# Transposes moved from TensorE to the DMA queue in a pooled-attention and mixture-of-experts kernel

## The chip, the core and the metric

The kernel runs on one core of a Trainium2 chip. The metric is the device time of one execution in microseconds, given as the median of the timed runs; one further execution was taken with the hardware profiler, and all rows of a profile come from it. In the profile PE is TensorE (PEld its weight loads), DVE is VectorE, ACT is ScalarE, POOL is GpSimd and SP is SyncE, which here does nothing but issue DMAs. "q" behind an engine's name (SPq) means its sequencer.

## The reference

Eight batches, 576 tokens each, 8 heads of 64. First attention over pooled keys: k and v are averaged over groups of 8 tokens, which leaves 72 of them. Its output x (512 wide) goes to a mixture of four attention experts with causal softmax, of which each token uses two.

```python
# attention over pooled k, v      (B, H, S, D) = (8, 8, 576, 64), pool = 8
k_p = k.reshape(B, H, Sp, pool, D).mean(axis=3)
v_p = v.reshape(B, H, Sp, pool, D).mean(axis=3)
attn = softmax(scale * q @ k_p.T)                  # 576 x 72 per head
x = (attn @ v_p) heads side by side                # (8, 576, 512)
# experts: E = 4, head width 64, the two best of four per token
logits = x @ w_gate
w = softmax of the two largest logits
for e in range(E):
    q, k, v = x @ wq[e], x @ wk[e], x @ wv[e]
    a = causal softmax(scale * q @ k.T)            # 576 x 576
    out += (w of e where e is among the two, else 0) * (a @ v @ wo[e])
```

## The kernel before

Each batch has 512 main tokens in four chunks of 128, and a tail of 64; the tails of two batches are worked on together. The work is cut into named units such as `5:x2` (batch 5, unit x2), each written as a Python generator, and `ORDER` (line 21) lists the units in the order in which they are emitted. A name that stands there twice or three times means the unit's next piece: usually PE's matmuls first, then the instruction that takes the result out of PSUM, then what follows (a mask, a store). Every instruction keeps its program order on its engine (`keep_in_program_order`, line 121, to which the profile therefore ascribes nearly everything), so each engine works through its own list, and an instruction that waits holds up all behind it on that engine. All DMAs are issued from SP's list, loads and stores alike. A DMA also waits until the DMA eight places ahead of it on that list has landed, since eight semaphores are used in turn.

The units that matter here:

- Loads `lk`, `lq`, `lv` (1 MB each per batch, two buffers of each) and the tails' loads `lkt`, `lqt`, `lvt`.
- `q0` to `q3` (`q_t`, line 357): four PE transposes of q per head pair into PSUM (`qT_ps`), one VectorE copy to `qT`. The main tokens lie with four consecutive tokens in one partition, and the transposes write into PSUM so that the order of the tokens is by chunk.
- `s0` to `s3` (`scores`, line 371): the scores against the pooled keys, and ScalarE's exponential into `etA`.
- `a0` to `a3` (`av`, line 384): the product with the pooled values into `oA_ps`, then on VectorE a reciprocal of the sums (`rzA`) and one multiplication for both heads that writes the chunk-wise `x_tm`.
- `x0` to `x3` (`x_t`, line 410): for every fourth column group `fc`, four PE transposes of x (with the permuted identity `perm`) into `xT_ps`, one VectorE copy of 128 x 512 into `xT`, which has two buffers.
- `p0` to `p3` (`proj`, line 458): the experts' q and k from `xT`; `v0` and `v2` (`values`, line 473): their v and the gate's logits.
- `g1` to `g6`: the gate. `g1` works on VectorE and ends with the mask of the two best; `g2` is one subtraction on POOL.
- `c00`, `c01`, `c10`, `c11`, `c2`: the experts' scores and their exponentials, with POOL's causal masks. `o0`, `o1` (`av`, line 607): the products with v for two experts each, and VectorE's scaling (`scaled`, line 547) into `o_sc`.
- `t0`, `t1` (`o_t`, line 633): four PE transposes of `o_sc` into `oT_ps` and one VectorE copy into `oT` (four buffers).
- `w0` to `w3`, `y0` to `y3` (`wo`, line 653): the output product from both `oT` of a batch, the copy from PSUM into one of three `ofin` buffers on ScalarE (w) or VectorE (y), and the store. `z0`, `z2` (`wo_two`, line 662) do the same for two chunks in the last batch.
- The tails' units: `qt`, `qx`, `sx`, `ax`, `xx`, `pt`, `vx`, `h0`, `h1`, `hd`, `ox`, `tx`, `w4`.
- `W:h0` to `W:h9` (`busy`, line 253): four matmuls on zeros whose result nobody reads.

At the start POOL zeroes four padded tiles, `etT`, two `etX` and `etD` (lines 198 to 200, through `persistent`, line 179), in which the tails' exponentials later fill only a part.

Of the kernel before, what the change touches and what calls it, by code (L numbers as in the profile page):

```python
# [21 lines left out]
0:lkb 0:lqb 0:lkt W:h6 W:h9 0:lvb W:h5 0:qcb1 0:ksb W:h2 0:lqa 0:kt 0:lva 0:qcb0 0:qca0 W:h3 W:h8  # L22
0:qca1 0:lvt 0:q3 0:q3 0:q2 0:lka 0:vsb W:h0 1:lkt 0:vsa 0:kpb 1:kt 0:q2 0:q1 0:kpb 0:q1 0:q0 1:lk
0:ksa 0:s2 0:kpa 0:q0 0:vt 0:kpa 0:vp 0:s2 1:lq 0:s1 0:s3 1:ks 1:qc W:lv 1:lv 0:vp 0:a2 W:h4 0:s1
0:a1 W:lq 0:a2 0:s3 0:a3 0:s0 1:kp W:h1 0:a1 0:s0 0:a3 0:a0 W:h7 1:kp 1:lvt 1:q2 0:a0 1:q0 1:q2 1:q0
0:lqt 1:q3 1:q1 1:q3 1:vs 1:s2 1:lqt 1:q1 1:s3 0:x1 0:x1 1:vt W:cv 0:x2 1:s0 0:x3 0:x2 1:qt 0:x3
1:s2 1:s0 0:x0 1:s3 1:s1 0:x0 0:v2 0:v2 0:v0 1:vp W:lk W:c2 2:lq 0:v0 1:vp 0:p2 0:g1 1:s1 W:c0 2:lkt
0:p2 1:a1 0:g2 2:lvt 1:a3 1:qx 2:lk 1:a2 W:c3 0:p0 1:a1 1:qx 2:lv 1:a3 W:c1 0:g3 1:a0 1:a2 0:p3 0:p0
1:sx 0:g4 0:g5 2:qc 0:p1 1:a0 0:p3 1:sx 0:c11 3:lq 0:c10 1:x2 0:p1 3:lkt 1:x1 1:x2 0:c11 1:x1 2:lqt
0:c2 1:x0 1:x0 1:x3 0:c10 1:ax 1:x3 2:q3 3:lqt 2:q3 3:lk 1:p2 2:kt 0:g6 0:c11 0:c2 2:vt 3:lv 0:c00  # L30
0:c01 2:q2 1:p2 0:c2 2:q0 0:c10 2:ks 0:c01 1:ax 2:q2 1:v0 2:q1 4:lkt 2:q0 1:v0 1:xx 0:o1 1:v2 2:q1
0:c01 1:xx 3:lvt 2:kp 1:v2 0:c00 2:kp 1:pt 0:o1 2:s0 2:s2 2:vs 1:vx 1:pt 2:s0 0:c00 0:t1 1:vx 1:g1
2:s1 2:s3 2:vp 0:t1 1:g2 2:s2 0:o0 1:p0 2:s3 2:vp 2:s1 3:kt 2:a3 2:a1 0:o0 2:a2 1:p0 3:qt 1:p3 1:p3
1:p1 2:a3 4:lq 3:qc 4:lk 2:a2 2:a1 2:a0 1:p1 1:c10 3:qx 1:c10 3:q1 2:a0 3:q1 3:ks 1:h1 3:qx 1:hd
2:x3 2:x2 1:h1 2:x3 2:x2 1:h0 1:hd 2:x0 2:x1 2:x0 1:c11 1:c00 3:vs 3:vt 2:x1 1:c10 3:q0 3:q3 3:q0
1:g3 1:h0 2:v0 1:g4 3:q3 3:kp 1:c11 3:kp 1:c00 2:v2 0:t0 3:s3 2:v0 0:t0 1:c2 3:q2 2:v2 3:q2 2:p0
1:c2 4:kt 3:vp 3:sx 2:p0 1:c01 2:p1 2:g1 3:s3 3:sx 5:lq 1:c01 3:vp 3:a3 1:hd 2:p2 3:ax 2:p1 3:a3
1:g5 2:p2 3:s1 3:s0 4:qc 1:c2 3:ax 4:q0 4:q0 1:g6 4:lv 3:s1 1:ox 4:lvt 1:ox 4:q1 1:c00 4:q1 3:s0
3:s2 3:s2 2:c01 4:ks 2:g2 1:c01 2:c00 4:q2 4:q2 3:xx W:lo 3:xx 3:a1 4:lqt 2:c01 3:a1 4:kp 3:pt 4:kp
3:a2 3:a2 2:c00 5:lkt 4:q3 3:a0 3:pt 1:o0 5:lqt 4:s1 5:lvt 2:p3 4:q3 3:a0 1:c11 3:x0 4:s1 2:p3 4:s0  # L40
4:s0 4:s2 5:qc 3:x1 1:o0 5:lk 3:x0 3:x1 4:s3 4:s3 5:q2 4:vs 4:vt 5:q2 1:t0 1:o1 5:vt 3:x3 2:g3 1:t0
3:x3 2:c2 3:x2 4:vp 3:x2 6:lvt 4:vp 2:c2 3:p1 1:o1 3:v0 2:c00 4:s2 2:c01 6:lkt 3:v0 5:lv 3:p1 5:q3
1:t1 2:c10 3:h0 1:t1 W:co 4:a1 2:c10 3:p3 4:a0 5:qt 5:q3 5:kt 3:p3 3:p2 3:p2 4:a1 5:qx 4:a0 2:c11
4:a3 5:q1 5:qx 2:g4 3:p0 3:h0 5:q1 4:a2 2:c10 2:c11 2:g5 0:w1 4:a3 3:p0 7:lkt 4:a2 3:c10 3:c11 5:ks
0:w1 5:kp 3:c10 4:x0 4:x0 3:v2 3:c11 5:kp 4:x2 4:x2 0:w0 2:c11 6:lq 2:c2 0:w0 3:c2 3:v2 5:s1 5:vs
# [12 lines left out]
4:g6 3:t1 5:g2 4:o1 7:s1 6:x2 7:qx 7:qx 4:o1 5:hd 5:h0 6:p2 7:q0 7:q0 7:sx 5:h1 5:c10 3:t0 6:p2 5:g3
7:sx 3:t0 6:p0 5:h1 7:a1 6:p3 6:v2 5:c10 4:o0 6:p3 1:w1 6:p1 7:a1 5:c10 6:v2 6:p0 3:tx 5:g4 7:a3
7:s0 4:o0 5:g5 3:tx 5:c2 6:p1 7:s0 3:y1 3:w4 7:a3 2:w1 2:w3 3:y1 7:ax 5:c2 7:a0 7:ax 3:w4 3:w0 7:a0  # L60
6:v0 3:y1 3:w0 3:w3 5:c00 5:g6 3:w3 7:x2 6:v0 5:c2 5:c01 7:x1 7:x2 7:x3 3:w4 5:c11 5:c00 7:x1 6:c10
4:t0 7:x3 5:c01 4:t0 5:c00 6:g1 5:ox 3:w0 7:xx 6:c2 5:c11 6:g2 6:c10 5:c01 5:c11 7:xx 6:c00 6:c2
7:vx 5:ox 5:o0 6:g3 7:vx 4:t1 4:t1 7:x0 6:c00 5:o1 7:x0 6:c10 4:w2 4:w2 7:p1 7:v0 5:o1 4:w2 5:o0
3:w3 7:p1 7:p3 4:y0 7:v0 7:p3 6:c11 6:c01 4:y0 4:y1 5:tx 6:c11 7:v2 6:c2 5:tx 3:w2 6:c01 4:y1 6:g4
7:p2 7:v2 6:c11 3:w2 6:c01 6:g5 7:p2 7:p0 6:g6 7:g1 5:t0 7:p0 7:c11 7:c10 6:c00 7:c10 5:t1 5:t0
7:c10 4:w3 6:o1 3:w2 5:t1 4:w3 7:c11 6:o0 7:g2 4:y0 5:w4 7:pt 6:o1 5:w4 5:y2 7:g3 7:c01 7:pt 6:o0
7:g4 4:y1 5:y2 7:c01 6:t0 6:t0 7:c2 6:t1 7:c2 7:g5 7:c11 7:g6 6:t1 4:w3 7:c2 5:y0 7:c00 5:w4 5:y0
5:y1 7:c00 7:h1 6:y1 5:y2 7:c01 5:y1 6:y1 5:y0 5:y1 7:c00 7:o1 7:h1 6:y1 6:w0 6:w0 7:o0 6:w0 5:w3
7:o1 7:t1 7:h0 5:w3 7:o0 7:hd 7:hd 7:t1 7:t0 7:h0 6:y3 7:t0 5:w3 7:z2 6:y3 7:hd 7:ox 6:y3 6:w2 7:z2
7:z0 7:ox 6:w2 7:tx 6:w2 7:tx 7:z0 7:w4 7:w4 7:w4  # L70
"""


@with_exitstack
def kernel(
# [103 lines left out]
    def persistent(name, count, shape, dtype, fills):  # L179
        bufs = []  # L180
        for i in range(count):
            t = const.tile(shape, dtype, name=f"{name}{i}")
            for pick, value in fills:
                nc.gpsimd.memset(pick(t), value)
            bufs.append(t)
        return bufs
# [82 lines left out]
    def part_a(b: int):  # L269
# [86 lines left out]

        def q_t(hp):
# [12 lines left out]

        def scores(hp):
            ps = ps2.tile([128, 2, MAIN], FP32, name="sA_ps", tag="ps2")
            for hh in range(2):
                r0 = hh * D
                pe.matmul(
                    out=ps[:, hh, :], lhsT=kp[r0 : r0 + D, hp, :],
                    rhs=st["qT"][r0 : r0 + D, hp, :], start=True, stop=True,
                )
            yield
            et = etp.tile([SP, 2, MAIN], BF16, name="etA", tag="etA")  # L380
            act.activation(out=et[:], in_=ps[0:SP, :, :], func=EXP, scale=ATT_EXP_SCALE)
            st["et"][hp] = et

        def av(hp):
# [4 lines left out]
            for hh in range(2):  # L389
# [10 lines left out]
            dve.reciprocal(out=rz[:], in_=view[:, :, :, D : D + 1])  # L400
            dve.tensor_tensor(
# [5 lines left out]
                op=MULT,  # L407
            )
# [31 lines left out]
        else:  # L440
# [5 lines left out]
            })  # L446
        units.update({f"{b}:{n}": f for n, f in names.items()})
# [4 lines left out]
    def part_p(b: int):  # L452
# [41 lines left out]
        def gate1():  # L494
# [72 lines left out]
    def part_s(b: int):  # L567
# [64 lines left out]

        def o_t(ep):
# [43 lines left out]
        for ep in range(NEP):  # L677
# [3 lines left out]
            names[f"t{ep}"] = lambda ep=ep: o_t(ep)  # L681
# [249 lines left out]
```

## Time and profile before

| | us |
|---|---|
| Median of 3 runs | 179.77 (179.53 to 181.32) |
| Profiled execution | 177.47 |
| its span from first to last instruction | 175.7 |
| TensorE's mean granted clock in it | 0.989 of full |

| What | Count | Mean, ns |
|---|---|---|
| PE transposes of x | 128 | 221 |
| PE transposes of the experts' output | 64 | 220 |
| VectorE copies into xT | 32 | 421 |
| VectorE copies into oT | 16 | 422 |
| POOL zeroing of etX, two tiles | 2 | 1906 |
| Stores of 256 KB, issue to landing | 28 | 2400 |

How to read it: the duration of a matmul in the profile is from its start to its modelled end, and matmuls follow each other much closer than that, so 221 ns is no price for a transpose. What a group of matmuls costs is read from the chain of waits or the timeline, where the next group's start shows when PE was free. "Idle before" is the time in which an engine had nothing to do ahead of an instruction, with what released it.

### The profile page before, as it was taken

What the parts mean: (1) busy time and instruction counts of PE and PEld (TensorE: products, weight loads), DVE (VectorE), ACT (ScalarE), POOL (GpSimd) and SP (SyncE); (2) the same over time, 40 slices, a digit from 0 to 9 for tenths busy, and PEclk for the clock granted to TensorE, in tenths of its full rate; (3) what the DMA queues carried; (4) which work ended last, traced back from release to release, by engine and by line L of the source; (5) the groups of instructions that cost most, each with busy time, mean ns of one, the idle gap of its engine ahead of it and who ended that gap; (6) DMA issues with size and microseconds to landing.
All of it is one profiled execution on the core that took longest, in us unless ns stands there. A gap on an engine that the chain in (4) does not pass through costs nothing.

```text
span 175.7 us, 5279 instructions
## 1 busy us (share of the span) xinstructions
PE 160.5 (91%) x2095; PEld 103.1 (59%) x2120; DVE 126.5 (72%) x357; ACT 124.1 (71%) x172; POOL 103.7 (59%) x212
## 2 busy tenths in 40 slices
PE   7849797999999999999999999999999999999680
PEld 2324455567667658676665687657666675575440
DVE  1586765867898767878777868786967877668650
ACT  2112647796669699787987798788796895798551
POOL 8963726369866999875789286982313171427000
PEclk9978999999999999999999999999999999999999
DMA  4999999999999999999947999352040503156566
GB/s 141 313 307 311 346 345 225 298 308 348 189 320 274 342 349 305 164 301 298 342 152 219 309 349 345 129 156 86 4 179 4 159 26 119 44 201 188 195 256 199
DMA packets 45208, 40.19 MB, mean 229 GB/s; under 512 B 14208, under 2 KB 40320, under 8 KB 45184
## 3 DMA queue, kind: packets, MB, share of 16 engines
q1 hardware_dynamic: 45184, 39.86, 78.1%
q8 instruction: 16, 0.26, 0.7%
q14 instruction: 8, 0.07, 0.1%
HBM read 30.42 MB, written 9.44 MB: 227 GB/s over the span
## 4 chain that ended last, share of the span: by engine, by line
PE 70%; SPq 12%; DMA 7%; ACT 5%; issue 2%; DVE 1%; POOL 0%; DVEq 0%; ACTq 0%; POOLq 0%
PE p_ps L121 16%; SPq L121 12%; PE v_ps L121 7%; PE y_ps L121 6%; PE sB_ps L121 6%; PE oB_ps L121 5%; DMA vtail<-in_v_dram 5%; PE oA_ps L121 4%; PE xT_ps L121 3%; PE sA_ps L121 3%; PE qT_ps L121 3%; PE oT_ps L121 3%; PE oBt_ps L121 2%; PE vp_ps L121 2%; PE pt_ps L121 2%
## 5 line engine op out<-in xcount | busy, mean ns | idle before, releaser
L121 ACT ACTIVATE etA<-sA_ps 72x1024 bf16<-72x1024 f32 x32 | 31.6, 1020 | 9.8 <-PE sA_ps L121 9.5
L121 ACT ACTIVATE etB<-sB_ps 128x1024 bf16<-128x1024 f32 x32 | 31.8, 1030 | 2.8 <-PE sB_ps L121 2.6
L121 PE MATMUL p_ps<-xT,wqk 128*128 128x512 bf16 x115 | 31.9, 379 | 0.8
L121 POOL TENSOR_SCALAR_AFFINE_SELECT etB<-etB 128x256 bf16<-128x256 bf16 x48 | 18.4, 406 | 21.2 <-ACT etB L121 21.0
L121 ACT CAST qk<-p_ps 128x512 bf16<-128x512 f32 x32 | 18.5, 586 | 10.8 <-PE p_ps L121 10.7
L121 POOL TENSOR_TENSOR vsum<-vraw 128x512 bf16<-128x512 f32 (+1 forms) x16 | 18.9, 1203 | 7.1 <-DMA vraw<-in_v_dram 5.3
L121 DVE TENSOR_TENSOR x_tm<-oA_ps,rzA 128x512 bf16<-128x512 f32 x32 | 22.1, 691 | 1.1
L121 PEld LDWEIGHTS <-wqk 128*128 128x128 bf16 x192 | 14.8, 98 | 9.7 <-issue 0.4
L121 POOL TENSOR_TENSOR ksum<-kraw 128x512 bf16<-128x512 f32 x14 | 17.5, 1271 | 2.2 <-DMA kraw<-in_k_dram 2.2
L121 PE MATMUL v_ps<-wvg,xT 128*128 128x260 bf16 x128 | 16.8, 274 | 0.4 <-DVE xT L121 0.2
L121 PE MATMUL y_ps<-wo_t,oT 128*128 128x512 bf16 x55 | 16.6, 379 | 0.3 <-DVE oT L121 0.3
L121 DVE COPY xT<-xT_ps 128x512 bf16<-128x512 bf16 x32 | 12.6, 421 | 5.4 <-PE xT_ps L121 5.1
L121 ACT COPY ofin<-y_ps 128x512 f32<-128x512 f32 x20 | 11.7, 589 | 6.7 <-PE y_ps L121 2.4
L121 DVE COPY qT<-qT_ps 128x512 bf16<-128x512 bf16 x32 | 13.1, 420 | 3.8 <-PE qT_ps L121 3.5
L121 POOL CAST qbf<-qraw 128x2048 bf16<-128x2048 f32 x7 | 13.2, 1890 | 2.9 <-PE sB_ps L121 1.5
L121 PE MATMUL qT_ps<-ident,qbf 128*128 128x128 bf16 x128 | 12.1, 224 | 3.0 <-DVE qbf L121 2.6
L121 PE MATMUL sB_ps<-qk 64*128 64x256 bf16 (+3 forms) x128 | 13.8, 300 | 0.3
L121 PEld LDWEIGHTS <-xT 128*128 128x128 bf16 x128 | 12.0, 97 | 3.3 <-DVE xT L121 0.5
L121 PEld LDWEIGHTS <-etA 72*128 72x128 bf16 x256 | 11.0, 97 | 4.9 <-issue 1.1
L121 PE MATMUL idle_ps<-idle 128*128 128x512 bf16 x39 | 11.9, 452 | 1.6 <-DVE idle L148 1.2
L121 PE MATMUL oA_ps<-vp,etA 72*128 72x65 bf16 x256 | 12.6, 194 | 0.3 <-DVE vp L121 0.2
L121 PEld LDWEIGHTS <-qbf 128*128 128x128 bf16 x128 | 8.1, 100 | 7.4 <-DVE qbf L121 3.1
(123 smaller groups left out, 338.7 us busy)
## 6 DMA issues: line engine op xcount, KB each, us to landing
kraw<-in_k_dram SPq DMA_DIRECT2D x7, 1024.0 KB, 8.5
qraw<-in_q_dram SPq DMA_DIRECT2D x7, 1024.0 KB, 9.8
vraw<-in_v_dram SPq DMA_DIRECT2D x7, 1024.0 KB, 10.2
out_dram<-ofin SPq DMA_DIRECT2D x28, 256.0 KB, 2.4
kraw<-in_k_dram SPq DMA_DIRECT2D x2, 512.0 KB, 5.9
qraw<-in_q_dram SPq DMA_DIRECT2D x2, 512.0 KB, 6.1
ktail<-in_k_dram SPq DMA_DIRECT2D x16, 64.0 KB, 7.3
vraw<-in_v_dram SPq DMA_DIRECT2D x2, 512.0 KB, 6.8
```

Source lines behind the costliest of these rows:

```text
L121: return tc.keep_in_program_order(fn(*args, **kwargs))
```

## The change

Three constants name the batches whose transposes go to the DMA queue. For batches 5, 6 and 7 the units `x0` to `x3` give way to `xd0` to `xd3`, one transposing DMA per chunk of 128 tokens, from `x_tm` (128 x 512) straight into `xT`, issued on SP. The DMA takes whole blocks of 128 columns, while `xT` needs every fourth column together; so `x_tm` is written in that arrangement, in two multiplications per head pair with strided output in place of one, and ScalarE's exponential writes `etA` in the order of the tokens (8 bytes between neighbours) while `q_t` leaves them as they lie. For batches 4 to 7 the units `t0` and `t1` become one transposing DMA each from `o_sc` into `oT`. The four padded tiles are zeroed on VectorE. The gate's mask moves from VectorE's `g1` to POOL's `g2`, in two operations. `ORDER` is a new arrangement of all units. `Q_BY_DMA` is empty, so that a third use, for q, stays unused.

SP issues 20 transposing DMAs more; PE has 4082 instructions in place of 4242.

```diff
 ORDER = """
-0:lkb 0:lqb 0:lkt W:h6 W:h9 0:lvb W:h5 0:qcb1 0:ksb W:h2 0:lqa 0:kt 0:lva 0:qcb0 0:qca0 W:h3 W:h8
...
-7:z0 7:ox 6:w2 7:tx 6:w2 7:tx 7:z0 7:w4 7:w4 7:w4
+0:lqb 0:lkb 0:lka 0:lkt W:h9 W:h6 W:h8 0:lqa 0:qcb1 W:h5 0:qcb0 0:q2 0:q2 0:ksb 0:kt 0:lvt 0:vt W:h0
...
+1:w3 5:a3 4:p0 3:g2 5:a0 1:w3 7:lk 3:g3 4:p1 5:a1 4:p1 5:xx 3:h1 3:c00 6:q3 5:a3 6:q3 3:h1 5:xx
+3:c00 5:xd2 4:v0 6:q1 4:c2 5:xd3 3:g4 6:q1 4:c2 5:pt 6:kp 4:v0 4:c01 5:pt 3:c01 6:q0 3:g5 3:o1 5:xd1
+6:kp 4:g1 5:xd0 1:tx 1:w3 4:c01 6:q0 7:lkt 2:t1 7:lvt 1:tx 6:s3 2:t1 3:c01 7:qc 7:q2 4:g2 4:g3 7:kt
+6:vp 7:q2 2:w0 6:s3 4:c00 6:vp 3:g6 2:w0 0:w2 6:s1 4:g4 6:s1 5:p3 5:p3 5:p2 0:w3 5:p2 3:ox 4:c00
...
+7:h1 6:w2 6:y3 7:h1 7:h0 5:w3 6:y3 7:t1 6:w2 7:t0 7:hd 6:y1 7:h0 6:y1 6:w2 6:w0 7:ox 7:z0 7:ox 6:y3
+7:tx 6:w0 6:y1 7:z2 7:tx 6:w0 7:w4 7:z0 7:z2 7:w4 7:w4
 """
+
+Q_BY_DMA = ()
+X_BY_DMA = (5, 6, 7)
+O_BY_DMA = (4, 5, 6, 7)
...
-    def persistent(name, count, shape, dtype, fills):
+    def persistent(name, count, shape, dtype, fills, eng=nc.gpsimd):
...
-                nc.gpsimd.memset(pick(t), value)
+                eng.memset(pick(t), value)
...
+    zeros = [(lambda t: t[:], 0.0)]
+    ett = persistent("etT", 1, [SP, 64 + 2 * H * 128], BF16, zeros, nc.vector)[0]
+    etx = persistent("etX", 2, [128, 2, 64 + 2 * NTC * 128], BF16, zeros, nc.vector)
+    etd = persistent("etD", 1, [128, 2, NEP, 128], BF16, zeros, nc.vector)[0]
...
                 pe.transpose(
-                    out=ps[:, :, r, :], in_=st["q"][:, r, 2 * hp : 2 * hp + 2, :],
+                    out=ps[:, r, :, :] if b in X_BY_DMA else ps[:, :, r, :], in_=st["q"][:, r, 2 * hp : 2 * hp + 2, :],
...
+                in_ = ps[0:SP, :, :].rearrange("s e (r p) -> s e r p", r=NR)
+                if b in X_BY_DMA:
+                    to = et[:].rearrange("s e (p r) -> s e r p", r=NR)
...
+            if b in X_BY_DMA:
+
+                x = st["x"][:].rearrange("p c (fc f) -> p c f fc", fc=NFC)
+                for hh in range(2):
+                    f0 = (2 * hp + hh) * (D // NFC)
+                    dve.tensor_tensor(
+                        out=x[:, :, f0 : f0 + D // NFC, :],
+                        in0=view[:, hh, :, 0:D].rearrange("p c (f fc) -> p c f fc", fc=NFC),
+                        in1=rz[:, hh].rearrange("p c (a o) -> p c a o", a=1).to_broadcast([128, NTC, D // NFC, NFC]),
+                        op=MULT,
+                    )
+                return
...
+        def x_dma(c):
+            sp.dma_start_transpose(
+                out=xT[:, :, c * 128 : c * 128 + 128], in_=st["x"][:, c, :]
+            )
...
-            dve.tensor_tensor(
-                out=g("g_msk", E)[:], in0=L[:], in1=m2[:].to_broadcast([128, NT, E]), op=ISGE
-            )
...
+            msk = g("g_msk", E)
+            pool.tensor_tensor(
+                out=msk[:], in0=gs["L"][:], in1=gs["g_m2"][:].to_broadcast([128, NT, E]), op=SUB
+            )
+            pool.tensor_scalar(
+                out=msk[:], in0=msk[:], scalar1=0.0, scalar2=None, op0=ISGE,
+            )
...
+        def o_dma(ep):
+            t = otp.tile([128, MAIN], BF16, name="oT", tag="oT")
+            sp.dma_start_transpose(
+                out=t[:].rearrange("p (c n) -> p c n", c=NTC),
+                in_=st["osc"].pop(ep)[:].rearrange("p c e d -> p (c e d)"),
+            )
+            st["oT"][ep] = t
...
-            names[f"t{ep}"] = lambda ep=ep: o_t(ep)
+            names[f"t{ep}"] = lambda ep=ep: (o_dma if b in O_BY_DMA else o_t)(ep)
```

In SP's new list the four DMAs of batch 5 stand behind the loads of q and k of batch 7 and ahead of its v and tails; those of batches 6 and 7 and all of `o_sc` stand among stores.

More of the change, by code (lines that the diff above doesn't have):

```diff
@@ new lines @@
+0:o0 3:kt 2:s2 3:qc 1:p3 2:s0 2:a3 1:p3 0:o0 2:a3 2:a0 2:a0 2:a2 1:p1 2:a2 1:p1 1:p0 3:ks 2:a1 3:lvt
+3:lqt 3:q1 1:p0 2:a1 3:vt 1:h0 0:t1 1:c2 1:c10 1:g3 3:lv 3:q1 4:lq 0:t1 4:lk 1:h0 1:c10 2:x2 2:x0
+2:x2 1:h1 2:x0 5:lq 2:x1 3:qt 1:h1 2:x3 1:c11 1:c2 2:x1 1:c11 2:x3 3:kp 2:p0 3:kp 2:p0 3:qx 1:c00
+1:c00 2:v2 3:q3 3:vs 1:g4 3:qx 3:q3 2:p1 4:qc 3:q2 4:lkt 2:v2 2:p1 3:sx 1:hd 3:q2 5:lkt 3:s3 1:g5
+3:vp 3:q0 3:vp 3:sx 2:v0 1:hd 0:t0 3:s1 3:q0 3:s3 1:c2 2:c01 3:s1 2:v0 0:t0 4:lv 4:q0 2:c01 1:hd
+3:ax 2:p2 4:q0 4:q1 3:a3 1:c00 3:ax 4:lqt 3:s0 4:ks 1:c01 4:q1 3:a3 2:p2 3:xx 1:ox 4:lvt 5:lqt 3:xx
@@ L355, in pool_v, with q_dma @@
             )
+        def q_dma():
+            t = apool.tile([128, NR, NHP, 128], BF16, name="qT", tag="qT")
+            sp.dma_start_transpose(
+                out=t[:].rearrange("p r hp n -> p (r hp) n"),
+                in_=st["q"][:].rearrange("p r h d -> p (r h d)"),
+            )
+            st["qD"] = t
         def q_t(hp):
@@ L374, in scores @@
                 r0 = hh * D
+                rhs = st["qD"][r0 : r0 + D, :, hp, :] if "qD" in st else st["qT"][r0 : r0 + D, hp, :]
                 pe.matmul(
-                    out=ps[:, hh, :], lhsT=kp[r0 : r0 + D, hp, :],
-                    rhs=st["qT"][r0 : r0 + D, hp, :], start=True, stop=True,
+                    out=ps[:, hh, :], lhsT=kp[r0 : r0 + D, hp, :], rhs=rhs, start=True, stop=True,
                 )
@@ L380, in scores @@
             et = etp.tile([SP, 2, MAIN], BF16, name="etA", tag="etA")
-            act.activation(out=et[:], in_=ps[0:SP, :, :], func=EXP, scale=ATT_EXP_SCALE)
+            to, in_ = et[:], ps[0:SP, :, :]
+            if "qD" in st or b in X_BY_DMA:
+                in_ = ps[0:SP, :, :].rearrange("s e (r p) -> s e r p", r=NR)
+                if b in X_BY_DMA:
+                    to = et[:].rearrange("s e (p r) -> s e r p", r=NR)
+                else:
+                    to = et[:].rearrange("s e (c r i) -> s e r c i", c=NTC, r=NR)
+                    in_ = in_.rearrange("s e r (c i) -> s e r c i", c=NTC)
+                if len(to.shape) == 5:
+                    for e in range(2):
+                        act.activation(out=to[:, e], in_=in_[:, e], func=EXP, scale=ATT_EXP_SCALE)
+                else:
+                    act.activation(out=to, in_=in_, func=EXP, scale=ATT_EXP_SCALE)
+            else:
+                act.activation(out=to, in_=in_, func=EXP, scale=ATT_EXP_SCALE)
             st["et"][hp] = et
@@ L446, in part_a @@
             })
+        if b in Q_BY_DMA:
+            names["qd"] = q_dma
+        if b in X_BY_DMA:
+            names.update({f"xd{c}": lambda c=c: x_dma(c) for c in range(NTC)})
         units.update({f"{b}:{n}": f for n, f in names.items()})
```

87 lines of the change are left out of this document (37 added, 50 removed).

## The prediction

> **What bounds the kernel now.** I read the page first, then busy time by stretch of the span, then what PE waited for, then the chain of waits.
>
> ```profile
> span 175.7 us, 5279 instructions
> PE 160.5 (91%) x2095; PEld 103.1 (59%) x2120; DVE 126.5 (72%) x357; ACT 124.1 (71%) x172; POOL 103.7 (59%) x212
> ```
> ```profile
> core 0: us, PE busy (x) PEld busy (x) DVE busy (x) ACT busy (x) POOL busy (x), PEclk, DMA share, GB/s
> 90.00:110.00 20.00, 19.84 (x303) 13.59 (x305) 16.12 (x51) 16.27 (x25) 13.74 (x25) 1.00 0.92 275
> 110.00:130.00 20.00, 19.74 (x272) 12.75 (x273) 15.55 (x49) 16.25 (x26) 10.81 (x23) 1.00 0.35 120
> 130.00:150.00 20.00, 19.82 (x261) 13.05 (x262) 15.41 (x46) 15.23 (x22) 6.23 (x21) 1.00 0.21 68
> 150.00:162.00 12.00, 11.80 (x154) 7.31 (x155) 8.65 (x27) 10.57 (x15) 5.99 (x20) 1.00 0.44 148
> ```
> ```profile
> PE oT_ps L121 <- ACT ofin L121: 1.3, 2, 1.0
> PE yt_ps L121 <- DVE oTt L121: 0.4, 1, 0.4
> PE y_ps L121 <- DVE oT L121: 0.3, 1, 0.3
> ```
>
> The DMA share is the last column but one: the queues are full up to about 110 us and mostly idle after it. PE has work in 71.2 of the 72 us from 90 to 162, at the full granted clock, and between 100 us and the end it waits 2.0 us in all (the last three rows, all in the tail). VectorE and ScalarE have about a fifth of their time free. Batches 5 to 7 therefore run at the pace of PE's list, and work taken off that list comes off the time, as long as what replaces it lands before PE asks for it.
>
> **The change, part by part. PE.** What leaves is 12 units of four transposes of x and 8 of four transposes of the experts' output: 80 transposes with their weight loads (4242 instructions on PE become 4082). Their price comes from the chain of waits, where a piece lasts until the next piece starts, and not from busy times, which overlap.
>
> ```profile
> 121.71 0.45 PE xT_ps L121 x8
> ...
> 130.21 0.86 PE p_ps L121 x4
> ...
> 132.18 0.90 PE v_ps L121 x8
> 133.08 0.61 PE oB_ps L121 x20
> ...
> 137.16 0.43 PE y_ps L121 x2
> ...
> 159.11 0.33 PE oT_ps L121 x4
> ```
>
> Back to back, eight transposes take 0.45, so 80 take 4.5. A lone unit of four takes 0.33, so 20 units take 6.6. In the old order about half stand alone: I take 5.5 off.
>
> **The new wait.** PE now meets the projection of batch b with xT written by four DMAs. How much PE work lies in between is counted in the new order from the rows above. Batch 6, from its last attention unit to its first projection: two projections (1.72), two value units (1.80), three output units (1.29), one experts' product (0.61), and 15 smaller units (transposes of q, scores, attention products, the pooling of v) at 0.22 to 0.65 with 4.7 in all, some 0.31 each like the lone unit above; 10.1 together. The same count gives 9.1 for batch 5 and 9.9 for batch 7. From it go VectorE's normalization of the last head pair and the landing of the last DMA.
>
> ```profile
> L121 DVE TENSOR_TENSOR x_tm<-oA_ps,rzA 128x512 bf16<-128x512 f32 x32 | 22.1, 691 | 1.1
> L121 DVE COPY xT<-xT_ps 128x512 bf16<-128x512 bf16 x32 | 12.6, 421 | 5.4 <-PE xT_ps L121 5.1
> L121 DVE RECIPROCAL rzA<-oA_ps 128x8 f32<-128x8 f32 x32 | 6.4, 199 | 3.6 <-PE oA_ps L121 3.5
> L121 DVE TENSOR_TENSOR o_st<-oBt_ps,gt 128x256 bf16<-128x256 f32 x4 | 1.7, 424 | 0.1
> L121 DVE COPY oTt<-oTt_ps 128x256 bf16<-128x256 bf16 x4 | 1.1, 282 | 0.9 <-PE oTt_ps L121 0.9
> L121 DVE TENSOR_TENSOR gt<-oB_ps,g_G 128x8 f32<-128x8 f32 x16 | 2.7, 167 | 0.9
> L154 DVE COPY perm<-ident 128x128 bf16<-128x128 bf16 x1 | 0.4, 367 | 0.3 <-POOL ident masks.py:199 0.3
> ```
> ```profile
> 168.47 1.06 SPq L121 DMA_DIRECT2D out_dram<-kraw  x2
> ```
> ```profile
> L121 SPq DMA_DIRECT2D out_dram<-ofin x36: 332/365/2802, 88.4 to 172.5; - x36
> ...
> DMA to landing us min/median/max: 2.0/2.4/9.2
> ```
> ```profile
> kraw<-in_k_dram SPq DMA_DIRECT2D x1, 1024.0 KB, 10.8
> ```
>
> The normalization is 0.20 and two halves like o_st's 0.42, 1.05; with 0.25 for the attention unit itself, 1.3. Landing is 2.2, between the least and the median of the stores. So four issues have 5.6 us in batch 5, 6.6 in batch 6, 6.4 in batch 7: 1.4 to 1.65 each. No transposing DMA is in this trace. A plain store costs SP 0.53 (the kraw row, two in 1.06) and the longest issue of one is 2.80. The true price lies between; I take 1.3, near the geometric middle, since 0.53 is for whole rows and a transposing DMA scatters each row over 128 partitions. At 1.3 all three batches just fit.
>
> [...]
>
> Batch 5 has one more trouble: its DMAs stand on SP's queue straight behind 1 MB of q and 1 MB of k of batch 7, while the queues are full. The row for such a load, between 98 and 106 us, says 10.8 to landing. If the transposes land 10.8 after x is ready, 12.1 stand against 9.1: 3 us of stall. If the loads have drained, none. I take 1.0. SP's other entries behind these DMAs are stores and the last tails and v of batch 7; in before SP spends 40.7 us waiting for ACT's ofin, as the next row says, so 12 issues of 1.3 have room.
>
> ```profile
> SPq L121 <- ACT ofin L121: 40.7, 13, 7.4
> ```
>
> **VectorE, ScalarE, POOL.** VectorE loses 20 copies (8.4) and eight small mask operations; it gains 12 times 2x0.424-0.691 = 0.16, which is 1.9. The new writes of x are strided. The one strided copy of the trace is perm: 0.37 for 128 elements, where the rows for 512 and 256 elements (0.421, 0.282) point to 0.21. That surplus of 1.2 ns an element would make 0.62 per head pair, 7.4 in all: it eats the saving, but VectorE is not the bound, and 0.3 of it (one half) falls on the path of each batch. Without a surplus it is 0; I take 0. [...] ScalarE's exponentials of batches 5 to 7 now write 8 bytes apart, 12 of 1024 elements.
>
> ```profile
> L121 ACT ACTIVATE etA<-sA_ps 72x1024 bf16<-72x1024 f32 x32 | 31.6, 1020 | 9.8 <-PE sA_ps L121 9.5
> ```
>
> Perm's surplus would add 1.2 us to each 1.02, the other end is nothing; I take nothing. POOL gets 16 small operations for the mask and has 9 of 20 us free from 110 us on. All of this is hidden as long as PE's list stays the longest; if ScalarE's end holds, it does not (a rival below).
>
> **Start.** The zeroing of the padded tiles goes from POOL to VectorE.
>
> ```profile
> L148 DVE MEMSET idle<- 128x256 uint32 x1 | 0.3, 272 | 0.9 <-PEq L915 0.9
> ```
> ```profile
> 5.00 0.76 DVE L121 TENSOR_TENSOR ksum<-kraw 128x256 bf16<-128x256 f32 x2 [3.15 <-DMA kraw<-in_k_dram]
> ```
> ```profile
> 6.23 3.76 POOL L184 MEMSET etX<- 128x2176 bf16 x2
> ```
> ```profile
> 6.95 4.31 DVE L121 CAST qbf<-qraw 128x512 bf16<-128x512 f32 x2 [1.19 <-DMA qraw<-in_q_dram]
> ```
> ```profile
> 10.79 0.62 PE L121 MATMUL qT_ps<-ident,qbf 128*128 128x128 bf16 x8 [2.60 <-DVE qbf L121]
> ```
> ```profile
> 21.96 8.33 DMA vtail<-in_v_dram
> ```
>
> At the idle row's rate (256 words in 0.27) the 3488 words of the four tiles take 3.7 us, which VectorE has before its first data at 5.0. Its two casts of q took 2.15 each beside POOL's zeroing, and PE waited 2.60 for them; without it they may be shorter. But the loads still come at the queues' pace, and the chain of waits runs through one of them until 30.3 us. So between -2.0 (most of PE's wait) and +0.5; I take -0.5.
>
> **Tail.** Batch 7's last output needs oT from DMA. From the end of PE's last main experts' product the new order holds 3.6 us of other PE work. The path is VectorE 0.20+0.17+0.69 (reciprocal, gate, scaling), issue 1.3, landing 2.2: 4.6, and up to 2.3 more where the other half's DMA or stores stand ahead on SP. That is a stall of 1.0 to 3.3 against the 2.0 of the tail's three rows above: -1.0 to +1.3, I take +0.5.
>
> Sum: -5.5 +1.0 -0.5 +0.5 = -4.5. The profiled execution took 177.47 (175.7 of span and 1.8 around it), so it would be 173.0; the median of the runs is 179.77, 2.3 above, and becomes **175.3**. With the ends of the terms its own range is 172 to 178.
>
> **The rivals.** *SP's issue is the bound* (slower). If a transposing DMA holds SP for t, each x batch waits 4t less its room, 12t-18.6 in all, and the tail about 2(t-1.3). The 5.5 are lost a little below t = 2.0. At t = 2.4: 10.2+2.2-5.5 = +6.9, 186.7. [...] Chance 0.20.
>
> *Only half lands in time* (no change). Batch 5 waits the whole 3 us behind the loads, the tail takes its +1.3 and start gives nothing: -5.5+3.0+1.3 = -1.2, 178.6. ScalarE leads to much the same: at 1.2 more per exponential its 58.3 busy us between 90 and 162 become 72.7 of 72, and it takes over from PE, about 179.8. For it: the 10.8; against it: before's waits show queues that are drained by 110 us. Chance 0.20.
>
> *The DMAs cost PE nothing and the order fits better*: -6.6-2.0, 171.2, within the forecast's own chance.
>
> **How the numbers follow.** Within 1% is 178.0 to 181.6, about what runs of this kernel can tell from no change (179.53 to 181.32 here). Forecast 0.57, all faster. No change 0.20. Slower 0.23: SP's rival 0.20, and 0.03 for a stall that none of these names. The range goes from 171.5 to 184, which takes in SP's rival up to t = 2.2 and leaves out its rest and little below.
>
> **What would show it.** PE's first projections of batches 5, 6 and 7 should follow the instruction ahead without a gap, or with about 1 us in batch 5; a gap in all three, with SP's issues longer than 1.65 us, is the slower rival; a gap in 5 alone, with landing near 10 us, is the load rival. ScalarE's exponentials of batches 5 to 7 should stay near 1.02 us, VectorE's halves of x at 0.42, its casts of q at the start fall below 2. PE should still be busy nine tenths up to the tail. A mean of SP's transposing issues above 2.0 us would make the prediction wrong in sign.

## The result and the profile after

The changed kernel takes 208.3 us (206.36 to 210.24, four runs) against 179.65 us for the kernel before beside it: 1.153 times as long, with a 95% interval of 1.139 to 1.167. The forecast was 175.3 and its range ended at 184. Some runs of a kernel are longer than its others, and a ratio rests on the shorter ones alone, here 206.36 and 206.6 (of `reads_both` below only 184.37); the profiled execution, 209.99 us with a span of 208.2, is one of the two longer ones.

The head of the page with PE's busy tenths and its granted clock in 40 slices of 5.2 us, and then the busy time by stretch, with the columns as in the prediction:

```profile
span 208.2 us, 5195 instructions
PE 169.7 (82%) x2040; PEld 104.3 (50%) x2040; DVE 136.5 (66%) x345; ACT 141.0 (68%) x172; POOL 103.9 (50%) x224
...
PE   7779689999999999959966987487767886897880
...
PEclk9969999999999999995888699979999999799998
```
```profile
90.00:110.00 20.00, 15.38 (x146) 9.09 (x145) 12.94 (x30) 13.91 (x13) 10.31 (x18) 0.77 0.59 185
110.00:130.00 20.00, 15.86 (x192) 9.84 (x190) 11.54 (x30) 14.69 (x16) 8.64 (x20) 0.89 0.55 142
130.00:150.00 20.00, 13.31 (x137) 8.30 (x139) 15.38 (x33) 14.41 (x15) 6.30 (x15) 0.91 0.44 122
```

Up to some 88 us (slice 17) PE is about as busy as in the kernel before. In the stretches after it PE, which was busy 19.7 to 19.8 of every 20 us there, has 13.3 to 15.9, and its granted clock, the third column from the end, falls to 0.77. No other engine has taken the bound over as a whole: VectorE is busy for 58 to 77% of these stretches and ScalarE for 70 to 73%. It is the chain from one to the other that sets the pace. What PE waited for, and then SP:

```profile
PE v_ps L125 <- DVE x_tm L125: 3.2, 2, 1.8
PE oA_ps L125 <- ACT etA L125: 2.9, 3, 1.0
PE oB_ps L125 <- ACT etA L125: 2.8, 2, 1.4
PE p_ps L125 <- ACT ofin L125: 2.6, 1, 2.6
```
```profile
SPq L125 <- ACT ofin L125: 24.5, 9, 6.2
SPq L125 <- DVE x_tm L125: 24.4, 2, 20.4
```

Two tiles stand there that PE never waited for in the kernel before: `x_tm`, which VectorE writes in the new arrangement, and `etA`, which ScalarE now writes with 8 bytes between neighbours. SP, meanwhile, stands up to 20.4 us in one place with everything else it has to issue behind it. The groups with their shapes kept apart, and the DMA issues with the median from issue to landing:

```profile
L125 ACT ACTIVATE etA<-sA_ps 72x1024 bf16<-72x1024 f32 x32 | 48.9, 1564 | 11.5 <-PE sA_ps L125 11.4
L125 DVE TENSOR_TENSOR x_tm<-oA_ps,rzA 128x256 bf16<-128x256 f32 x24 | 29.3, 1410 | 0.5
```
```profile
L125 SPq DMA_TRANSPOSE xT<-x_tm x12: 1195/1257/1311, 114.1 to 171.4; - x12
```
```profile
xT<-x_tm SPq DMA_TRANSPOSE x12, 2.5
oT<-o_sc SPq DMA_TRANSPOSE x8, 2.3
```

The exponentials have a mean of 1564 ns over 32. Twenty are as before (1018, from the run `reads_both` below), so the twelve of batches 5 to 7 take (32x1564 - 20x1018)/12 = 2.47 us each. VectorE's halves take 1.41 us; a head pair's two overlap and hold the engine 29.3/12 = 2.44 us, where one full instruction took 0.69. The transposing DMAs themselves are as forecast: 1.26 us of SP, 2.5 us to landing. The chain of waits shows how the slow writes join, here around batch 6's attention:

```profile
114.09 1.80 PE v_ps L125 x8
...
121.06 2.33 ACT etA L125
...
129.14 2.46 DVE x_tm L125 x2
...
131.64 0.43 PE oA_ps L125 x8
132.10 0.22 DVE rzA L125
132.34 2.45 DVE x_tm L125 x2
...
134.84 0.63 PE oA_ps L125 x8
```

PE's attention products need a free PSUM buffer, that buffer waits for VectorE's multiplication (2.46 and 2.45 us for a head pair here), and the next product stands behind it on PE's list. One more thing can be read here: `v_ps` x8, behind a wait of 1.8 us, took 1.80, and 0.90 in the kernel before. The granted clock is 0.57 and 0.58 in the two stretches of 2 us from 114 on, and 1.00 again from 118 to 120. So a wait can be paid a second time behind it. Not every wait is: from 140 to 170 us PE is busy 6.6 to 8.1 of every 10 us, at a clock of 1.00.

### The profile page after: what moved, and what is told of

It reads as the page before. It is cut to its first block, busy times and chain, and to the rows that moved or that the text cites. A ratio compares the mean times of both kernels' runs of the same rounds, so it can differ in the third digit from the quotient of the medians.

```text
span 208.2 us, 5195 instructions
## 1 busy us (share of the span) xinstructions
PE 169.7 (82%) x2040; PEld 104.3 (50%) x2040; DVE 136.5 (66%) x345; ACT 141.0 (68%) x172; POOL 103.9 (50%) x224
## 4 chain that ended last, share of the span: by engine, by line
PE 41%; DVE 20%; DMA 15%; ACT 12%; SPq 5%; issue 4%; POOL 1%; DVEq 0%; ACTq 0%
DVE x_tm L125 14%; PE p_ps L125 9%; ACT etA L125 6%; PE v_ps L125 6%; SPq L125 5%; DMA qraw<-in_q_dram 4%; DMA out_dram<-ofin 4%; DMA wk_f<-in_moe_wk_dram 4%; PE sB_ps L125 3%; DMA kraw<-in_k_dram 3%; PE y_ps L125 3%; PE oA_ps L125 2%; PE xT_ps L125 2%; PE sA_ps L125 2%; PE qT_ps L125 2%
## 5 line engine op out<-in xcount | busy, mean ns | idle before, releaser
L125 ACT ACTIVATE etA<-sA_ps 72x1024 bf16<-72x1024 f32 x32 | 48.9, 1564 | 11.5 <-PE sA_ps L125 11.4
L125 DVE TENSOR_TENSOR x_tm<-oA_ps,rzA 128x256 bf16<-128x256 f32 (+1 forms) x44 | 43.2, 1083 | 1.2
L125 PE MATMUL p_ps<-xT,wqk 128*128 128x512 bf16 x128 | 34.0, 394 | 2.7 <-ACT ofin L125 2.6
L125 POOL TENSOR_SCALAR_AFFINE_SELECT etB<-etB 128x256 bf16<-128x256 bf16 x48 | 18.5, 408 | 13.7 <-ACT etB L125 13.3
L125 PE MATMUL v_ps<-wvg,xT 128*128 128x260 bf16 x128 | 19.6, 303 | 4.4 <-DVE x_tm L125 3.2
L125 PE MATMUL y_ps<-wo_t,oT 128*128 128x512 bf16 x64 | 19.9, 410 | 0.6 <-ACT ofin L125 0.6
L125 DVE COPY qT<-qT_ps 128x512 bf16<-128x512 bf16 x32 | 13.8, 437 | 9.5 <-PE qT_ps L125 9.5
L125 PEld LDWEIGHTS <-xT 128*128 128x128 bf16 x128 | 13.2, 108 | 9.6 <-DVE x_tm L125 3.9
L125 PE MATMUL oB_ps<-vaug,etB 128*128 128x65 bf16 x256 | 12.9, 197 | 2.8 <-ACT etA L125 2.8
L125 PEld LDWEIGHTS <-etB 128*128 128x128 bf16 x256 | 12.1, 99 | 4.6 <-issue 3.1
L125 PEld LDWEIGHTS <-qk 64*128 64x128 bf16 x256 | 7.3, 95 | 12.6 <-issue 5.4
```

Of the source, the lines that this page charges most:

```text
L125: return tc.keep_in_program_order(fn(*args, **kwargs))
```

## The experiments

Theory A said that the scattered writes are the loss: ScalarE's, VectorE's, or both. The rival (B) was that something else of the change is, SP's list above all, and the slow writes only lie beside it.

**plain**: both writes contiguous again, so x reaches `xT` in another arrangement than the projections want.

```diff
-            if "qD" in st or b in X_BY_DMA:
+            if "qD" in st:
...
-            if b in X_BY_DMA:
+            if False:
```

> The changed kernel, but ScalarE's exponential and VectorE's normalization of batches 5 to 7 use the old, contiguous patterns (one multiplication per head pair); tokens and columns of these batches are therefore not brought into the order that the DMA transposes need, which leaves the rearrangement out. Theory A (the scattered 2-byte writes are the loss: 12 exponentials 1.3 us longer, 12 head pairs 1.8 us longer, and all that waits for them): the time falls to what the prediction forecast for everything else, 173 to 178 us, SP's transposing issues stay near 1.26 us and PE's clock returns to 0.98 or more. Rival B (SP's list is the loss: a transposing DMA that waits for x holds up the loads behind it, 20 us once): the time stays above 190 us.

**reads_both**: the same values in the same places, but the stride stands on the side of the read from PSUM.

```diff
-                    to = et[:].rearrange("s e (p r) -> s e r p", r=NR)
+                    to = et[:].rearrange("s e (p r) -> s e p r", r=NR)
+                    in_ = ps[0:SP, :, :].rearrange("s e (r p) -> s e p r", r=NR)
...
-                x = st["x"][:].rearrange("p c (fc f) -> p c f fc", fc=NFC)
+                x = st["x"][:].rearrange("p c (fc f) -> p c fc f", fc=NFC)
...
-                        in0=view[:, hh, :, 0:D].rearrange("p c (f fc) -> p c f fc", fc=NFC),
+                        in0=view[:, hh, :, 0:D].rearrange("p c (f fc) -> p c fc f", fc=NFC),
```

> The changed kernel with the same values in the same places, but the stride moved from the written to the read side: ScalarE reads PSUM 512 bytes apart and writes etA contiguously, VectorE reads PSUM 16 bytes apart and writes runs of 16 elements. Theory A1 (only scattered writes to SBUF are slow): exponentials back to 1.02 us, halves of x to 0.42 us, time 174 to 179 us. Theory A2 (a stride is slow on either side): exponentials stay near 2.3 us, halves near 1.25 us, time 200 to 210 us. Rival B: above 190 us whatever these durations are.

**reads_dve** and **reads_act**: only VectorE's half of this edit, and only ScalarE's.

> As the run with both strides on the read side, but for VectorE's multiplications alone; ScalarE still writes 8 bytes apart. Theory A1: halves of x 0.42 us, exponentials 2.3 us; of the 29 us lost about 12 x 1.8 = 21 us of VectorE time go, some of which was beside PE's work, so 182 to 194 us. If VectorE's writes were hidden and ScalarE's were the loss, above 200 us.

> As the run with both strides on the read side, but for ScalarE's exponentials alone; VectorE still writes 256 bytes apart. Theory A1: exponentials 1.02 us, halves of x 1.25 us; 12 x 1.3 = 16 us of ScalarE time go, so 190 to 200 us. If ScalarE's writes were the whole loss, below 182 us.

Measured: plain 185.96 (184.64 to 188.55), reads_both 187.29 (184.37 to 187.66), reads_dve 198.21 (195.48 to 201.44), reads_act 200.49 (199.33 to 201.71), with 178.97 for the kernel before. The groups of reads_both:

```profile
L125 ACT ACTIVATE etA<-sA_ps 72x1024 bf16<-72x1024 f32 x32 | 31.7, 1018 | 9.4 <-PE sA_ps L125 9.2
L125 DVE TENSOR_TENSOR x_tm<-oA_ps,rzA 128x256 bf16<-128x256 f32 x24 | 9.0, 419 | 0.4
```

Both are back at the times that the prediction had taken, 1.02 and 0.42. The strided writes cost 21 us by the medians and 22.0 by the lowest runs (206.36, 184.37), and the same stride on the read costs nothing that can be seen: the values are the same, and so is the number of instructions, and plain, which leaves the rearrangement out, is no faster (lowest run 184.64). With one half mended 11 to 15 us of the loss stay, so the two overlap in part. All four times are longer than theory A had put (reads_act by 0.5 us), and the first two are shorter than B's. 187.3 is still 8 above the kernel before (7.5 by the lowest runs, 184.37 and 176.91), so a second loss is left. Its place is in reads_both's waits of PE, and in a stretch of its chain:

```profile
PE p_ps L125 <- ACT ofin L125: 6.0, 3, 3.8
```
```profile
113.44 0.59 ACT ofin L125
...
114.05 0.54 SPq L125
...
114.64 4.93 DMA out_dram<-ofin
...
119.67 0.59 ACT ofin L125
...
120.31 1.02 PE p_ps L125 x4
```

ScalarE copies an output out of PSUM, the store is issued and lands, and only then has ScalarE a free buffer for the next: PE's projection waits for the store of an earlier batch. SP's list in the same run shows why it was late:

```profile
101.49 5.79 SPq L125 DMA_TRANSPOSE xT<-x_tm  x4
107.38 0.53 SPq L125 DMA_DIRECT2D out_dram<-ofin  x1
107.96 1.32 SPq L125 DMA_DIRECT2D ktail<-in_k_dram  x2
...
110.67 1.57 SPq L125 DMA_DIRECT2D out_dram<-ofin  x3
```

Theory C: the stores are shut in behind DMAs that wait for x, and three output buffers do not carry that. Rivals: the transposes come late by themselves (D), or the new order doesn't fit (E).

**deep_stores**: five output buffers; two of them come from the weights' staging tiles, which are free by then.

```diff
-            t = ofp.tile([128, DM], FP32, name="ofin", tag="ofin")
+            t = ofin()
...
+    def ofin():
+        if next(turn) % 5 < 3:
+            return ofp.tile([128, DM], FP32, name="ofin", tag="ofin")
+        return wstage.tile([128, DM], FP32, name="ofin", tag="wstage")
```

> The kernel with both strides on the read side (187.3 us, 8 above the kernel before) and five output buffers in place of three: two of every five come from the weights' staging tiles, which are free by then. Theory C, stores shut in: SP's list runs in order, a store stands behind a transposing DMA that waits for x, ScalarE finds no free output buffer, its evictions stop and PE's projections wait for it (6.0 us of PE in three waits on ofin, and half speed after each). Two more buffers carry about two such waits: 176 to 181 us, PE's waits on ofin under 2 us. Theory D, the transposes come late by themselves: the waits on ofin were only a place where the lateness shows, and PE then waits for oT or xT instead: 184 to 188. Theory E, the new order does not fit whatever the stores do: 184 to 188, with waits spread over many tiles.

**pool_stores**: three buffers, `pool.dma_start` in place of `sp.dma_start` in `store`.

> Strides on the read side; all stores are issued by GpSimd, so SP's list keeps loads and transposing DMAs alone. Three output buffers as before. Theory C: no store waits behind a transpose any longer, PE's waits on ofin go, 176 to 182 us, less what GpSimd loses by waiting for outputs ahead of its masks (a wait of PE for masked tiles would show that). Theory D: 184 to 188, PE waits for xT or oT. Theory E: 184 to 188. Above 190 would say that GpSimd's own list became the bound and the run tells nothing on C.

**x_only** (`O_BY_DMA = ()`) and **o_only** (`X_BY_DMA = ()`), three buffers; the PE units stand where the DMA units stood or at the next place with a free PSUM buffer.

> Strides on the read side; x of batches 5 to 7 by DMA, the experts' outputs by PE again (32 transposes back on PE, 1.8 to 2.6 us of PE). Theory C: the x DMAs are those that wait on SP with stores behind them (issue 1.26 us each and a wait for x), so most of the loss stays: 183 to 187. Theory D with the outputs' DMA late in the tail as cause: 178 to 181. Theory E: 185 to 189.

> The experts' outputs of batches 4 to 7 by DMA, x by PE again (48 transposes back on PE, 2.7 to 4 us of PE, and contiguous writes of x). Theory C: eight transposing DMAs stand on SP with stores behind them in the last 50 us, a part of the loss stays, 180 to 184. Theory D with x as cause: 176 to 180. Theory E: 185 to 189.

Measured, with 179.18 before: deep_stores 179.08 (ratio 0.996, 0.990 to 1.003), pool_stores 202.22 (1.126), x_only 185.37 (1.034), o_only 182.57 (1.017). Two buffers give back 8.2 us by the medians and 5.9 by the lowest runs (184.37, 178.44), as C said, and PE's waits for ScalarE's `ofin` fall from the 6.0 in three to 0.4 in one. Half speed did not follow each of the three: in reads_both PE's granted clock is 1.00 from 110 to 150 us, where `p_ps` x4 takes 1.02 us behind the store above, and 0.72 from 150 to 162, where x6 takes 2.76. x_only came out as C had it (and within E's range, which deep_stores rules out), o_only within C's range. pool_stores was a bad test, as its waits of GpSimd and of PE show:

```profile
POOL g_w L125 <- ACT g_ex L125: 10.4, 5, 7.7
```
```profile
PE y_ps L125 <- ACT ofin L125: 8.4, 3, 5.8
PE oT_ps L125 <- ACT ofin L125: 6.7, 1, 6.7
```

GpSimd's list waits too, once 7.7 us for ScalarE in the gate, and the stores were shut in there. By its expectation a time above 190 tells nothing on C; it looks like the same fault on another list.

deep_stores, 179.1, is level with the kernel before where 4.5 us less were forecast. Its busy time by stretch, and its chain:

```profile
110.00:130.00 20.00, 18.36 (x247) 11.73 (x249) 13.02 (x44) 15.65 (x24) 12.20 (x27) 1.00 0.91 234
130.00:150.00 20.00, 18.80 (x268) 11.92 (x268) 13.23 (x44) 17.80 (x25) 8.16 (x27) 1.00 0.56 107
```
```profile
109.33 0.65 SPq L125
110.02 2.52 DMA ktail<-in_k_dram
...
113.72 6.44 DMA vraw<-in_v_dram
120.23 2.50 POOL vsum L125 x2
122.77 0.59 PE vp_ps L125 x3
```

The DMA share from 110 to 130 was 0.35 before and is 0.91: batch 7's v and tails are loaded there, since they stood on SP behind batch 5's transposes until 109. In the kernel before the last of them was issued by 105. PE waited only 0.4 us for `xT` here, so the room for x's DMAs was enough. Theory F: put them ahead, and the rest comes back. **loads_deep** does that with five buffers, **loads_ahead** with three; **before_deep** and **before_zero** are controls, the kernel before with five buffers, and with the zeroing on VectorE.

```diff
-3:c00 5:xd2 4:v0 6:q1 4:c2 5:xd3 ...
+3:c00 7:lkt 7:lvt 7:lv 7:lqt 6:lqt 5:xd2 4:v0 6:q1 4:c2 5:xd3 ...
```

The five units are taken out of their old places, in lines further down.

> Five output buffers and reads strided (179.1 us), and the last loads (tails of batches 6 and 7, v of batch 7) stand on SP's list ahead of batch 5's four transposing DMAs, not behind. In the run with five buffers these loads were issued at 109 to 119 us, behind four DMAs that waited for x until 102.5; in the kernel before they were issued at 93 to 102; PE was busy 18.4 and 18.8 of 20 us in the two stretches from 110 to 150, and the chain ran through ktail, vraw and the sum of v to PE at 122.8. Theory F, the loads shut in: PE is busy 19.6 of 20 there, 175 to 177.5 us, near the forecast's 175.3. Rival G, the x DMAs' own waiting (batch 5's room is too small): the gap moves to a wait of PE for xT, 178.5 to 180.

> The same order of loads with three output buffers. If stores and loads behind the waiting DMAs are two separate losses, the loads alone give back about 2.5 to 3 of 187.3: 183.5 to 185.5, with PE's waits on ofin still there (4 us or more). If the loads were what shut the stores in, most of the loss goes: 176 to 180.

> The kernel before with five output buffers and nothing else: a control. PE waited for an output buffer 1.3 us in two waits, both in the tail. Theory C says that the buffers help only where stores are shut in: 178 to 179.5, against 179.2. If buffers are scarce in any order, 174 to 177, and the gain of the run with five buffers says nothing on the change.

> The kernel before with the padded tiles zeroed on VectorE, the start of the change alone, in the old order. The forecast gave it -0.5 (from -2.0 to +0.5): 178.7 (177.2 to 179.7). VectorE's casts of q should take 0.45 in place of 2.15. If the loads set the pace of the start, no change in time although the casts are fast.

Measured, with 178.53 before: loads_deep 182.87 (1.028, 1.022 to 1.034), loads_ahead 187.57 (1.054), before_deep 177.39 (0.994, 0.990 to 0.999), before_zero 176.98 (0.995, 0.991 to 0.999). Theory F fell: the order that serves the loads is slower, with three buffers too, where the loads alone gave nothing back (183.5 to 185.5 had been expected at most). before_deep lies between its two expectations: five buffers alone gain the kernel before 0.6%, about 1 us, so that much of what deep_stores gained isn't the stores that were shut in. What PE waited for in loads_deep:

```profile
PE p_ps L125 <- DMA xT<-x_tm: 6.3, 2, 5.3
```

That is rival G, stronger than it was put. The loads and their waits hold SP until 106.2 us, and x's DMAs, whose x VectorE had written by 102.3, stand behind that. Theory H, then: one list cannot serve both. Rival I: the order is slower by itself. **loads_pool** issues the same loads from GpSimd, whose own operations free their buffers; **x67_deep** transposes batch 5's x on PE (`X_BY_DMA = (6, 7)`); **order_pe** has every transpose on PE in the new order; **zero_deep** is the kernel before with both controls' edits. All have five buffers.

> Reads strided, five output buffers (179.1 us); the last loads (tails of batches 6 and 7, v of batch 7) are issued by GpSimd, whose own operations set their buffers free, so that SP's list has neither loads behind batch 5's four transposing DMAs nor transposing DMAs behind loads. Theory H, one in-order list cannot serve both: PE waits under 1 us for xT and is busy over 19.5 of 20 us from 110 to 150; 175 to 177.5 us. Theory I, the order is slower by itself or the DMAs' own time is too long: 178.5 to 181. Above 182: issuing on GpSimd costs more than the list.

> Reads strided, five output buffers; x of batch 5 is transposed by PE, that of batches 6 and 7 and the outputs by DMA. 16 transposes return to PE, 0.9 to 1.3 us. Theory H: the collision of batch 5 with batch 7's loads was the only one, since no loads are left behind batches 6 and 7: about 2.8 less 1.1, 176.5 to 178.5. Theory I: 179 to 181, the transposes added and nothing won.

> The rearranged order, five output buffers, zeroing on VectorE, and every transpose on PE as before (contiguous writes, no transposing DMA): the order alone. It stands against the kernel before with five buffers (177.4) and the start (-1.5 by its own run). Theory H: the order is as good as the old one, 175.5 to 178.5, no PE wait above 1 us from 90 to 150. Theory I: 179.5 to 184, with waits although no DMA is in the way.

> The kernel before, old order, with zeroing on VectorE and five output buffers. Each alone gave about 1.1 to 1.5 (ratios 0.994 and 0.995). If they add up: 175.5 to 176.8. If both remove the same wait: 176.8 to 178.

Measured, with 178.20 before: loads_pool 183.06 (1.029), x67_deep 177.02 (0.995, 0.992 to 0.999), order_pe 184.25 (1.035), zero_deep 177.13 (0.992, 0.988 to 0.996). x67_deep came out in H's range. In loads_pool SP's list was free of these loads and PE waited for xT all the same. The DMAs issued from 100 to 116 us, and what PE waited for:

```profile
vraw<-in_v_dram POOLq DMA_DIRECT2D x1, 1024.0 KB, 8.8
...
xT<-x_tm SPq DMA_TRANSPOSE x4, 8.6
```
```profile
PE p_ps L125 <- DMA xT<-x_tm: 4.4, 2, 3.6
```

The same four in deep_stores, in the same stretch, where these loads were not yet issued:

```profile
xT<-x_tm SPq DMA_TRANSPOSE x4, 3.1
```

183.06 is also above the 182 from which the expectation spoke of a cost of issuing on GpSimd. PE's waits for GpSimd don't show one (4.0 us in all, 3.5 in deep_stores), but the run can't rule it out.

So H had the place right and the cause wrong. The list is one bottleneck, and by their share the DMA engines behind it are a second: in the three stretches of 4 us from 104 to 116 it is 1.04, 1.22 and 1.07 in loads_pool, where the transposing DMAs land in 8.6 us beside 1.5 MB of loads (`vraw` in 8.8), and 0.73, 0.50 and 0.85 in deep_stores, where they land in 3.1. Batch 5's x and batch 7's loads fall in the same 15 us, and in these runs whichever went first, the other was late (a wait of 5.3 us for `xT` in loads_deep, `vraw` on the chain for 6.44 in deep_stores). x67_deep takes the collision away:

```profile
110.00:130.00 20.00, 19.55 (x269) 12.76 (x274) 14.56 (x49) 17.39 (x26) 10.89 (x24) 1.00 0.64 185
```

PE is busy again from 110 to 130, 19.55 for 18.36. Against deep_stores the gain is small: the medians differ by 2.1, but 1.0 of it is the difference between the two times of the kernel before beside them, and the ratios (0.995 and 0.996) overlap. What batch 5's DMA saved on PE it cost in the collision, or a little more; these runs put it no closer.

order_pe speaks for I, but not cleanly. The new order with all transposes on PE is 7.1 us slower than the old order with the same buffers and start (zero_deep), a little more than I had put, but without the waits that I had named: there is no wait over 0.5 us from 90 to 162, and PE is busy 67.5 of those 72 us (71.2 in zero_deep). That order was arranged without these units and they were put back by a rule, so part of it may lie there. How much belongs to the order itself stays open. Whether the two edits of zero_deep add up can't be told either (0.992, against 0.994 and 0.995 for one alone).

Two runs on what the outputs' DMA brings beside x of batches 6 and 7: **tail_pe** (`O_BY_DMA = (4, 5, 6)`) and **x67_alone** (`O_BY_DMA = ()`).

> As the kernel of 177.0 us (reads strided, five output buffers, x of batches 6 and 7 and the outputs by DMA), but batch 7's outputs transposed by PE: 8 transposes back, 0.45 to 0.66 us, against a landing of about 2.4 us on the chain of the tail. If the DMA in the tail costs what the forecast said (+0.5) or more: 175.5 to 177. If it costs nothing or is a gain: 177 to 178.

> The same with the outputs of all batches by PE, only x of batches 6 and 7 by DMA: 32 transposes back on PE, 1.8 to 2.6 us. If the outputs' DMA is hidden: 178.5 to 179.8. If its waits and issues cost what it saves: 176.5 to 178.

Measured, with 177.63 before: tail_pe 177.25 (0.997, 0.993 to 1.001), x67_alone 180.04 (1.013, 1.009 to 1.017). By the ratios the outputs' DMA is worth 1.7%, 3.1 us, more than the 2.6 at most that had been expected, and in the tail it makes no difference that these runs can tell.

## Why the prediction was wrong

- **The step that failed: strided writes at nothing.** "I take nothing" for ScalarE and "I take 0" for VectorE, and a surplus was called hidden as long as PE's list stays the longest. They cost 1.45 us per exponential (bound: 1.2), and a head pair takes 2.44 (taken: 0.85, bound: 0.85+0.62); together 21 us of time, not hidden, since PE waits for `etA` and `x_tm`. The bounds came from perm's copy, most of whose surplus was not its stride. In before_zero, where VectorE does the zeroing itself, the three rows that bear on it read:

```profile
L121 DVE CAST qbf<-qraw 128x512 bf16<-128x512 f32 x2 | 0.9, 428 | 4.1 <-DMA qraw<-in_q_dram 4.1
L184 DVE MEMSET etX<- 128x1088 uint32 x2 | 1.9, 965 | 0.4 <-issue 0.4
L154 DVE COPY perm<-ident 128x128 bf16<-128x128 bf16 x1 | 0.2, 246 | 0.0
```

  Perm takes 0.25 in place of 0.37 with the same stride, and the cast of q 0.43 in place of 2.15. Beside VectorE's zeroing one GpSimd operation (a select into `pmt`) now takes 2.23 us in place of 0.25. So at the start operations of one engine took longer beside those of the other, in both traces; why, no run shows.
- **The rival that came near.** "ScalarE takes over from PE, about 179.8" had one of the two mechanisms, at 0.20 with another. It took ScalarE's load against 72 us of busy time. But the slow operations of batch after batch stand in one chain with PE, and the wait counts there, not the free share of an engine: ScalarE was busy 14.7 of 20 us at most in the stretches above.
- **The second step that failed: SP "has room".** The 40.7 us in which SP waited for outputs were read as slack. SP works in order: while it waited for x, 20.4 us at once in the change, it issued nothing from 93.7 to 114.1 us, and three output buffers were enough only as long as it didn't wait for anything but outputs. This cost 6 to 8 us (about 1 of which five buffers gave the kernel before too), and no rival named it.
- **Batch 5 behind the loads, +1.0 (0 to 3).** The collision is real: x landing after 8.6 us (loads_pool), a wait of 3.6 us. In the change's own order it was the loads that lost, and the step put the wait at the wrong tile: at PE's v pooling, not at xT. By x67_deep its price is about 0 to 1 us more than what the 16 transposes save, which is within the noise.
- **The DMAs' price.** Issue 1.3 and landing 2.2 were taken, 1.26 and 2.5 or 2.3 measured. The 1.3 is in part luck: its lower bound, 0.53 for a plain store, is half of a merged row with a pause in it, and each of these two issues took 0.33, from which the same middle would have been 0.96. With 1.26 measured the slower rival, SP's issue at 2.0 or more, is out: the right sign for a wrong reason.
- **PE, -5.5 for 80 transposes.** From order_pe to x67_deep, measured side by side, 64 transposes are worth 7.2 us against 4.4 at that price. So the price was not too high, but part of the 7.2 is the copies' waits in that order.
- **Start, -0.5.** before_zero: 0.995, 0.9 us. Right in sign, within its bounds: the casts are fast, and the second then waits for its load, as the row above shows. **Tail, +0.5:** tail_pe can't tell it from nothing. **The range of the terms, 172 to 178,** is narrower than their ends, which add up to 170.2 and 180.1.

So with the writes mended and the buffers added the change comes out level with the kernel before (0.996), and with the kernel before with five buffers (0.994). What is missing from the forecast's 4.5 us is in part the collision of batch 5; the rest would be the new order, by order_pe, and of that the share is open. From 90 to 162 us PE is busy 68.8 of 72 us in deep_stores and 68.7 in x67_deep, against 71.2 in the kernel before: batches 5 to 7 no longer run at the pace of PE's list alone. The mask on GpSimd was not tried by itself. The lowest ratio is zero_deep's, the old order with the change's start and five buffers, 0.992; before_deep (0.994), before_zero (0.995) and x67_deep (0.995) can't be told from it, so no run shows that the transposing DMAs gain anything over the old order with these two small edits.

## What to carry to other kernels

When a layout has to change between PSUM and SBUF, put the stride on the read from PSUM and write SBUF in runs (here the strided reads cost nothing that shows, the strided writes 21 us); price a strided write from a row of the same engine, undisturbed, and not from a neighbour's (perm's copy, the row taken here, was 0.37 us in the kernel before and 0.25 in before_zero). A DMA that waited for a computed tile, here 20.4 us, stopped all that stood behind it on its list: before putting one there, list the loads and stores behind it and count the buffers that bridge its wait. And moving the loads to another list did not help here (183.1 us against 179.1): beside 1.5 MB of loads in flight the transposing DMAs landed as late as the loads (8.6 and 8.8 us).

## What the hardware showed that was not expected

- A bf16 write with 8 bytes between neighbours took ScalarE 2.4 times as long (1024 elements: 2.47 us in the change against 1.02 in reads_both), and one with 256 bytes between neighbours took VectorE 3.4 times as long (256 elements a partition: 1.41 against 0.42). VectorE's copy of 128 elements at 8 bytes paid next to nothing (0.246 us in before_zero, where its contiguous copies of 256 and 512 point to 0.21). In reads_both fp32 reads from PSUM cost neither engine anything, VectorE's at 16 bytes between neighbours (0.419 us; `o_st`, of the same size, 0.424) and ScalarE's at 512 (1.018; 1.020 in the kernel before).
- Transposing DMAs of 128 x 512 bf16 landed in 2.3 to 3.1 us without these loads beside them (medians of the change, reads_both, deep_stores and x67_deep) and in 8.6 beside 1.5 MB of loads (loads_pool).
- After some waits PE ran at half speed: `v_ps` x8 in 1.80 us against 0.90, at a granted clock of 0.57. In loads_deep the clock is 0.50 from 112 to 116 us and 0.70 from 116 to 120, behind the wait of 5.3 us, and `p_ps` x8 takes 3.57 us, where x4 took 0.86 ahead of it. Such a wait cost PE more than its length: 0.90 us more in the change, and in loads_deep 1.85 (3.57 less two times 0.86).
